# Joining the value products of one tile and the score products of a later one in a single TensorE run, in halves of two PSUM banks

## The chip, the core and the metric

The kernel runs on one core of one Trainium2 chip. The metric is the device time of one execution in microseconds (us). Five engines work from queues of their own, each in order: TensorE (PE) multiplies matrices from SBUF into PSUM, VectorE (DVE), ScalarE (ACT) and GpSimd (POOL) do the element-wise work, SyncE (SP) issues most of the transfers.

## What is computed

Three layers follow each other. The shapes are 8 batches, 8 heads, 576 positions, 64 columns per head; 4608 tokens of 512 columns; hidden widths 1024 and 2048.

```python
# attention inside chunks of 64 positions, q, k, v: (8, 8, 576, 64)
scores = scale * np.matmul(q_c, k_c.transpose(0, 1, 2, 4, 3))
attn = np.exp(scores - np.max(scores, axis=-1, keepdims=True))
attn = attn / (np.sum(attn, axis=-1, keepdims=True) + 1e-09)
x = np.matmul(attn, v_c)                      # then (4608, 512)
# SoLU layer, w_in (512, 1024), w_out (1024, 512)
h = x @ w_in
e = np.exp(h - h_max)
solu = h * (e / (np.sum(e, axis=-1, keepdims=True) + 1e-09))
ln = (solu - mu) / np.sqrt(var + 1e-06) * g_ln
x = ln @ w_out
# leaky layer, w_in (512, 2048), w_out (2048, 512)
h = x @ w_in
out = np.maximum(0.01 * h, h) @ w_out
```

## The kernel before

The first stretch of the kernel does the attention and the SoLU layer in 36 tiles of 128 tokens (`T = 36`); the second does the leaky layer, six groups of 768 tokens, and is not touched. Beside the first stretch, ACT, DVE and POOL also prepare the weights of the later layers piece by piece.

The order of the work is written out by hand: no scheduler moves anything, each engine's queue is in the order in which the loop (L743 to L860) calls the helpers. One round t of the loop (also called tile t below) works on several tiles at once:

- `load_qk(t + 3)` and `load_v(t + 2)` (L756, L757) put transfers on SP's queue.
- `qk_mm(t + 2)` (L347) makes the scores of the tile two ahead: 16 products of 64 x 64 x 64 in the program, 32 records in the trace (s_ps).
- `solu_max(t - 1, 1)` and `solu_a(t - 1)` (L472, L477): row maximum of the second half of the hidden block on DVE (L475), then two exponentials on ACT (L483).
- `softmax_a(t + 2)` (L367): row maximum of the scores (L372) and their subtraction (L373) on DVE, the exponential on ACT (L379).
- `ff1_mm(t, 0)` (L444): first half of the hidden block, 12 products of 512 columns (h_ps, L460). Its last four read the low part of x.
- `solu_b(t - 1)` (L487) on DVE: products L491, which are the last readers of tile t - 1's hidden block. Three PSUM banks hold the halves of hidden blocks in turn, so the second half of tile t gets the bank that the first of these products frees.
- `pt_mm(t + 1)`, `softmax_b(t + 2)`, `pt_copy(t + 1)`: transposes of the probabilities, sum and division, copy on ACT (L402).
- `take_magnitudes`, `convert_a`, `convert_b`: weight pieces, ACT L103, DVE L110 to L120. A round takes one piece, and two in the rounds of `DOUBLE` (5, 6, 7, 14, 15, 22, 23, 30, 31).
- `y1_group` (L552): 24 products of the output of the SoLU layer (y_ps), one group per round from round 5 on.
- `attend(t)` (L580): `pv_mm(t + 1)` (L406) makes the values (x_ps, again 32 records), `x_split(t + 1)` copies their high part on ACT (L437) and makes their low part on DVE (L442).
- `lnT_mm(t - 2)` and `lnT_split` (L525, L541): eight transposes of the normalised block, and their high (ACT L546) and low (DVE L550) parts. These PSUM banks (tag "ef", two of them) are also those of `y1_group`, in turn.
- `ff1_mm(t, 1)`: second half of the hidden block.
- `finish` (L241): of pairs of converted pieces a block is folded and split (L179 to L198): POOL L191 and L192, DVE L193 and L194, ACT L196, POOL L197.

In every fourth round (5, 9, 13, ... 33; `late` in the code) the transposes of the normalised block come ahead of the second half, and `attend` and the output group come last. Rounds 6 to 8, 10 to 12 and so on have the order above.

Scores and values have PSUM tiles with the same tag, "s", of which there is one, two banks wide (`two_banks`, L78). They take turns: the scores are read by DVE before the values of the same round are made, and the values are read by `x_split` before the next scores.

Of the kernel before, what the change touches and what calls it, by code (L numbers as in the profile page):

```python
# [18 lines left out]
B, H, S, D = 8, 8, 576, 64  # L19
# [4 lines left out]
T = NT // P  # L24
NB = NT // 512
KD = DM // P
# [16 lines left out]
AHEAD = 5  # L43
# [9 lines left out]
def kernel(  # L53
# [21 lines left out]
    def bank(tag, name):  # L75
        return (ps2 if tag == "ef" else ps1).tile([P, 512], F32, tag=tag, name=name)

    def two_banks(name):  # L78
        return ps1.tile([P, 2, 512], F32, tag="s", name=name)
# [210 lines left out]
    def w_load():  # L290
        at = next(w_order, None)
        if at:
            w = ws.tile([P, 2, 2 * P], F32R, tag="w", name="w_s")
            sync.dma_start(out=w.bitcast(F32), in_=wi_d[at[0]][:, w_place[at[1]]])
            w_tiles.append(w)
# [12 lines left out]
    with tc.manual_schedule():  # L308

        with ExitStack() as phase:  # L310
# [17 lines left out]
            def load_qk(t, eng=sync):  # L328
                if t >= T:
                    return  # L330
                qt[t] = pa.tile([P, KD, P], F32, tag="qt", name="qt")
                eng.dma_start(out=qt[t], in_=q[t])
                eng.dma_start(out=kbs[t % 2], in_=k[t])

            def load_v(t):
                if t >= T:
                    return
                for r in range(2):
                    for e in range(2):
                        sync.dma_start(  # L340
                            out=vs[t % 2][r * D : (r + 1) * D, 2 * e : 2 * e + 2],
                            in_=v[t, e * D : (e + 1) * D, r::2],
                        )

            s_ps = {}

            def qk_mm(t):  # L347
                if t == 1:
                    ps = [bank("ef", "s_ps") for e in range(2)]
                    s_ps[t] = ps = [x.rearrange("p (h n) -> p h n", h=H)[:, :KD] for x in ps]  # L350
                else:
                    both = two_banks("s_ps").rearrange("p e (h n) -> p e h n", h=H)[:, :, :KD]
                    s_ps[t], ps = both, [both[:, e] for e in range(2)]
                kb, qq = kbs[t % 2], qt.pop(t)
                for i in range(KD):
                    for e in range(2):
                        r = slice(e * D, (e + 1) * D)
                        for c in range(2):
                            pe.matmul(  # L359
                                ps[e][c * D : (c + 1) * D, i, :],  # L360
                                lhsT=qq[r, i, c * D : (c + 1) * D],
                                rhs=kb[r, i, c, :],
                                start=True,
                                stop=True,
                            )

            def softmax_a(t):  # L367
                ps = s_ps.pop(t)
                sm = st8[t] = pa.tile([P, 2, H], F32, tag="st8", name="st8")
                e = es[t] = pa.tile([P, H, D], F32, tag="es", name="es")  # L370
                top = sm[:, 0].rearrange("p (e i) -> p e i", e=2)
                dve.reduce_max(top, ps, axis=AX)  # L372
                dve.tensor_tensor(  # L373
                    e.rearrange("p (e i) n -> p e i n", e=2),
                    ps,
                    top.unsqueeze(3).to_broadcast([P, 2, KD, D]),
                    op=ALU.subtract,
                )
                act.activation(e, e, AF.Exp, scale=scale)  # L379
# [23 lines left out]

            x_ps = {}

            def pv_mm(t):  # L406
                if t == 1:
                    ps = [bank("ef", "x_ps") for r in range(2)]
                    ps = [x.rearrange("p (a n) -> p a n", a=KD)[:, :2] for x in ps]
                    x_ps[t] = [(r, x) for r, x in enumerate(ps)]  # L410
                else:
                    both = two_banks("x_ps").rearrange("p r (a n) -> p r a n", a=KD)[:, :, :2]
                    ps = [both[:, r] for r in range(2)]
                    x_ps[t] = [(slice(0, 2), both)]
                vv, pp = vs[t % 2], pt.pop(t)
                for a in range(2):
                    for c in range(2):
                        for r in range(2):
                            k = slice(r * D, (r + 1) * D)
                            for e in range(2):  # L420
                                pe.matmul(  # L421
                                    ps[r][e * D : (e + 1) * D, a, c * D : (c + 1) * D],
                                    lhsT=vv[k, 2 * e + a, c],
                                    rhs=pp[k, 2 * e + a, c * D : (c + 1) * D],
                                    start=True,
                                    stop=True,
                                )

            def x_split(t):
                x_hi(t)  # L430
                x_lo(t)

            def x_hi(t):
                x = xs[t] = pa.tile([P, 2, KD, P], F32R, tag="xs", name="xs")
                hi = x[:, 0].rearrange("p (a r) n -> p r a n", a=2)
                for r, ps in x_ps[t]:
                    act.activation(hi[:, r], ps, AF.Copy)  # L437

            def x_lo(t):
                hi, lo = (xs[t][:, e].rearrange("p (a r) n -> p r a n", a=2) for e in range(2))  # L440
                for r, ps in x_ps.pop(t):
                    dve.tensor_tensor(lo[:, r], ps, hi[:, r].bitcast(F32), op=ALU.subtract)  # L442
# [29 lines left out]
            def solu_max(t, n):  # L472
                if n == 0:
                    sol[t] = wk.tile([P, 12], F32, tag="z", bufs=3, name="z")
                dve.reduce_max(sol[t][:, 8 + n : 9 + n], hs[t, n], axis=AX, negate=True)  # L475

            def solu_a(t):  # L477
                z = sol[t]
                dve.tensor_tensor(z[:, 0:1], z[:, 8:9], z[:, 9:10], op=ALU.min)  # L479
                u = us[t] = wk.tile([P, FF1], F32, tag="us", bufs=3, name="us")  # L480
                for n in range(2):
                    c = slice(n * 512, (n + 1) * 512)
                    act.activation(  # L483
                        u[:, c], hs[t, n], AF.Exp, bias=z[:, 0:1], accum_out=z[:, 8 + n : 9 + n]
                    )
# [93 lines left out]

            def attend(t):  # L580

                pv_mm(t + 1)
                x_split(t + 1)


            start = ExitStack()
# [66 lines left out]
            def warm(n):  # L653
                for _ in range(n):
                    pe.transpose(spare[:, :P], ident, ident)

            qk_mm(0)
            load_qk(2)
            load_next(2)
# [12 lines left out]
            magnitude(4)  # L672
            warm(14)
            qk_mm(1)
            maxima(0)
            exponentials(0)
# [10 lines left out]
            pt_copy(0)  # L687
            warm(6)
            pv_mm(0)
            maxima(1)  # L690
            exponentials(1)
# [5 lines left out]
            warm(6)  # L697
            ff1_mm(0, 0)
            qk_mm(2)
            factors(1)  # L700
            high(5)
# [6 lines left out]
            magnitude(8)  # L708
            pt_copy(1)
            pv_mm(1)  # L710
            convert(7)
            low(6)
# [30 lines left out]
            for t in range(1, T + 2):  # L743
                if t == T:
# [8 lines left out]
                        y_load(0, n)  # L753
                    for _ in range(WS):
                        w_load()
                load_qk(t + 3)  # L756
                load_v(t + 2)  # L757
                store_next()
                load_next(owed)
# [8 lines left out]
                    groups = [(NB - 1, m) for m in range(KD)]  # L768
                late = g == 0 or t == T - 1
                pieces = 0 if t < AHEAD or t >= T - 2 else 2 if t in DOUBLE else 1  # L770
                if t + 2 < T:
                    qk_mm(t + 2)
                if 1 <= t <= T:
                    if t < 3:
                        solu_max(t - 1, 0)
                    solu_max(t - 1, 1)
                    solu_a(t - 1)
                if t + 2 < T:
                    softmax_a(t + 2)
                if t > AHEAD and not late:  # L780
                    take_magnitudes(pieces)
# [39 lines left out]
                if groups and not late:  # L821
                    for bm in groups:
                        y1_group(*bm)
                    if t + 1 < T:
                        attend(t)
# [7 lines left out]
                else:  # L833
# [4 lines left out]
                    if t == 1:  # L838
                        ff1_mm(t, 1, (2,))
                        attend(t)  # L840
                        ff1_mm(t, 1, (3,))
                    elif t < T - 1 and not late:
                        attend(t)
# [202 lines left out]
        for g in range(NG):  # L1046
# [17 lines left out]
            for s in range(SLOTS):  # L1064
                p, i = divmod(s, PAIRS)
# [93 lines left out]
```

## Time and profile before

| | |
|---|---|
| median of 3 runs | 1241.79 us (1241.59 to 1242.41) |
| profiled execution | 1242.7 us, span of the profile 1240.9 us |
| mean granted clock of TensorE | 0.994 of full speed |
| busy: PE, DVE, ACT, POOL | 1218.2, 892.8, 572.0, 285.9 us |
| rounds 6 to 33, the stretch of the change | from 87.39 to 477.16 us of the span |
| one round there | 13.91 us, 13.96 us in every fourth |

Times in the trace are in us from the start of the span. A timeline row gives the start, the duration, engine, source line, operation, what is written and read, and how many records follow each other; an idle stretch before it stands in brackets with what ended it. The ends of products on PE are modelled, so starts are compared with starts.

### The profile page before, as it was taken

What the parts mean: (1) busy time and instruction counts of PE and PEld (TensorE: products, weight loads), DVE (VectorE), ACT (ScalarE), POOL (GpSimd) and SP (SyncE); (2) the same over time, 40 slices, a digit from 0 to 9 for tenths busy, and PEclk for the clock granted to TensorE, in tenths of its full rate; (3) what the DMA queues carried; (4) which work ended last, traced back from release to release, by engine and by line L of the source; (5) the groups of instructions that cost most, each with busy time, mean ns of one, the idle gap of its engine ahead of it and who ended that gap; (6) DMA issues with size and microseconds to landing.
All of it is one profiled execution on the core that took longest, in us unless ns stands there. A gap on an engine that the chain in (4) does not pass through costs nothing.

```text
span 1240.9 us, 22946 instructions
## 1 busy us (share of the span) xinstructions
PE 1218.2 (98%) x8554; PEld 1073.5 (87%) x8554; DVE 892.8 (72%) x1536; ACT 572.0 (46%) x1079; POOL 285.9 (23%) x388
## 2 busy tenths in 40 slices
PE   5999999999999999999999999999999999999998
PEld 3778878887887878899889989998999899889987
DVE  7789778878987886436785776577657766775675
ACT  6655546545654555433533442353344333443451
POOL 0266557666765664100000000000000000000000
PEclk8899999999999999999999999999999999999999
DMA  7435465654856574279889888988997898789676
GB/s 251 141 117 156 162 207 186 238 176 165 274 175 210 167 246 145 94 264 303 278 285 315 270 242 297 308 253 264 296 305 240 264 306 294 240 267 295 189 228 197
DMA packets 153790, 288.84 MB, mean 233 GB/s; under 512 B 14288, under 2 KB 63440, under 8 KB 152656
## 3 DMA queue, kind: packets, MB, share of 16 engines
q1 hardware_dynamic: 153312, 286.78, 71.8%
q8 instruction: 69, 1.13, 0.4%
q10 hardware_dynamic: 368, 0.59, 0.1%
q14 instruction: 41, 0.34, 0.1%
HBM read 239.08 MB, written 48.23 MB: 232 GB/s over the span
## 4 chain that ended last, share of the span: by engine, by line
PE 94%; DVE 4%; ACT 1%; DMA 0%; POOL 0%; issue 0%; POOLq 0%
PE h_ps L902 28%; PE o_ps L959 19%; PE y_ps L562 16%; PE h_ps L460 15%; PE o_ps L970 10%; PE ln_ps L535 2%; PE x_ps L421 2%; PE s_ps L359 1%; PE pt_ps L396 1%; DVE wf L116 1%; DVE wf L120 0%; DVE us L491 0%; DVE z L475 0%; DMA raw<-in_w_in 0%; DVE wf L112 0%; DVE wf L110 0%
## 5 line engine op out<-in xcount | busy, mean ns | idle before, releaser
L902 PE MATMUL h_ps<-yo,w_s 128*128 128x384 f32 x2016 | 351.0, 334 | 0.0
L902 PEld LDWEIGHTS h_ps<-yo,w_s 128*128 128x128 f32 x2016 | 349.3, 188 | 0.7
L959 PE MATMUL o_ps<-wo_s,yo 128*128 128x512 f32 (+1 forms) x1016 | 262.9, 393 | 0.0
L460 PE MATMUL h_ps<-wi,xs 128*128 128x512 f32 x864 | 219.9, 404 | 3.5 <-DVE xs L442 2.3
L562 PE MATMUL y_ps<-lnT,wo 128*128 128x512 f32 (+1 forms) x888 | 205.5, 388 | 0.2 <-DVE lnT L550 0.2
L959 PEld LDWEIGHTS o_ps<-wo_s,yo 128*128 128x128 f32 x1016 | 179.0, 188 | 28.7
L460 PEld LDWEIGHTS h_ps<-wi,xs 128*128 128x128 f32 x864 | 158.9, 190 | 38.3 <-DVE xs L442 2.6
L562 PEld LDWEIGHTS y_ps<-lnT,wo 128*128 128x128 f32 x888 | 161.1, 188 | 32.6 <-DVE lnT L550 0.4
L970 PEld LDWEIGHTS o_ps<-wo_s,yo 128*128 128x128 f32 x1008 | 144.6, 188 | 15.6
L273 DVE TENSOR_TENSOR yo<-c,yo 128x768 fp32r<-128x768 f32 x144 | 132.4, 951 | 32.0 <-ACT yo L272 32.0
L970 PE MATMUL o_ps<-wo_s,yo 128*128 128x256 f32 x1008 | 149.7, 283 | 0.0
L881 ACT ACTIVATE c<-h_c 128x384 f32<-128x384 f32 x144 | 72.9, 526 | 127.3 <-DVE h_c L913 127.3
L913 DVE TENSOR_TENSOR h_u<-h_ps,h_p 128x384 f32<-128x384 f32 x96 | 53.2, 554 | 106.7 <-PE h_ps L902 99.9
L272 ACT ACTIVATE yo<-c 128x768 fp32r<-128x768 f32 x144 | 113.0, 835 | 7.1 <-DVE c L943 5.5
L483 ACT ACTIVATE us<-h_ps,z 128x512 f32<-128x512 f32 x72 | 48.7, 682 | 48.9 <-DVE z L479 48.9
L386 POOL TENSOR_TENSOR es<-es,st 128x512 f32<-128x512 f32 x33 | 34.5, 1044 | 154.4 <-ACT pt L402 80.1
L272 ACT ACTIVATE yo<-a 128x768 fp32r<-128x768 f32 x36 | 29.9, 837 | 72.5 <-DVE a L267 72.5
L475 DVE TENSOR_REDUCE z<-h_ps 128x1 f32<-128x512 f32 x72 | 48.9, 681 | 19.7 <-PE h_ps L460 19.6
L913 DVE TENSOR_TENSOR h_c<-h_ps,h_u 128x384 f32<-128x384 f32 x96 | 53.1, 553 | 12.8 <-PE h_ps L902 12.3
L570 ACT ACTIVATE ys<-y_ps 128x512 f32<-128x512 f32 x36 | 21.4, 593 | 87.6 <-PE y_ps L562 86.5
L881 ACT ACTIVATE c<-h_ps 128x384 f32<-128x384 f32 x48 | 23.6, 492 | 76.2 <-PE h_ps L902 76.2
L550 DVE TENSOR_TENSOR lnT<-ln_ps,lnT 128x512 fp32r<-128x512 f32 x72 | 45.9, 680 | 12.4 <-ACT lnT L546 12.4
(86 smaller groups left out, 1399.4 us busy)
## 6 DMA issues: line engine op xcount, KB each, us to landing
w_s<-wi_d SPq DMA_DIRECT2D x336, 256.0 KB, 4.0
wo_s<-wo_d SPq DMA_DIRECT2D x168, 512.0 KB, 4.6
wi_d<-wi SPq DMA_DIRECT2D x8, 1792.0 KB, 6.0
wo_d<-wi SPq DMA_DIRECT2D x8, 1792.0 KB, 7.0
raw<-in_w_out SPq DMA_DIRECT2D x24, 512.0 KB, 6.1
raw<-in_w_in SPq DMA_DIRECT2D x23, 512.0 KB, 5.1
vs<-in_v SPq DMA_DIRECT2D x144, 64.0 KB, 3.8
a<-y_d SPq DMA_DIRECT2D x24, 384.0 KB, 5.2
```

Source lines behind the costliest of these rows:

```text
L272: act.activation(o[:, 0], x, AF.Copy)
L273: dve.tensor_tensor(o[:, 1], x, o[:, 0].bitcast(F32), op=ALU.subtract)
L460: pe.matmul(hs[t, n], lhsT=x[:, a, kk, :], rhs=w[:, b, kk % 2, n, :], start=(kk == 0 and a == 0 and b == 0), stop=(kk == KD - 1 and a == 1),)
L475: dve.reduce_max(sol[t][:, 8 + n : 9 + n], hs[t, n], axis=AX, negate=True)
L483: act.activation(u[:, c], hs[t, n], AF.Exp, bias=z[:, 0:1], accum_out=z[:, 8 + n : 9 + n])
L550: dve.tensor_tensor(dst[:, 1], ps, dst[:, 0].bitcast(F32), op=ALU.subtract)
L562: pe.matmul(ps[:, part], lhsT=w[:, a, kk % 4, m * P : (m + 1) * P], rhs=lnT[:, c, kk, pairs, :][:, part], start=(kk == 0 and a == 0 and c ...
L881: act.activation(blocks[block, j // 2][:, j % 2], src, AF.Prelu, alpha=0.01)
L902: pe.matmul(ps, lhsT=w[:, a, kk * P : (kk + 1) * P], rhs=y[:, c, kk, :], start=(first and kk == 0 and a == 0 and c == 0), stop=(kk == 1 an ...
L913: dve.tensor_tensor(o, ps, x, op=ALU.add)
L959: pe.matmul(ps[:, : 2 * P * (a.stop - a.start)], lhsT=x[:, 0, kk, m * P : (m + 1) * P], rhs=w[:, kk, a].rearrange("p a n -> p (a n)"), sta ...
L970: pe.matmul(sums[p % 2][m][:, : 2 * P], lhsT=x[:, 1, kk, m * P : (m + 1) * P], rhs=w[:, kk, 0], start=False, stop=(i == PAIRS - 1 and kk = ...
```

## The change

From round 5 to round 32, `attend(t)` takes the two banks once, as `xs_ps`. `pv_mm(t + 1)` writes its values in the upper 256 columns of both banks, `qk_mm(t + 3)` right behind it the scores of the tile three ahead in the lower 256. Then come `x_split(t + 1)` and `softmax_a(t + 3)`. The calls of `qk_mm(t + 2)` and `softmax_a(t + 2)` at the head of the round remain for rounds up to 5 only. Queries and keys are loaded one tile earlier from round 6 on, and at round 5 for two tiles.

```diff
-            def qk_mm(t):
+            def qk_mm(t, both=None):
...
-                    both = two_banks("s_ps").rearrange("p e (h n) -> p e h n", h=H)[:, :, :KD]
+                    both = two_banks("s_ps") if both is None else both
+                    both = both.rearrange("p e (h n) -> p e h n", h=H)[:, :, :KD]
...
-            def pv_mm(t):
+            def pv_mm(t, both=None):
...
-                    both = two_banks("x_ps").rearrange("p r (a n) -> p r a n", a=KD)[:, :, :2]
+                    both = two_banks("x_ps") if both is None else both
+                    both = both.rearrange("p r (a n) -> p r a n", a=KD)[:, :, 2:]
...
             def attend(t):
 
-                pv_mm(t + 1)
-                x_split(t + 1)
+                if AHEAD <= t < T - 3:
+                    both = two_banks("xs_ps")
+                    pv_mm(t + 1, both)
+                    qk_mm(t + 3, both)
+                    x_split(t + 1)
+                    softmax_a(t + 3)
+                else:
+                    pv_mm(t + 1)
+                    x_split(t + 1)
...
-                load_qk(t + 3)
+                load_qk(t + 3 if t <= AHEAD else t + 4)
...
-                if t + 2 < T:
+                if t <= AHEAD:
                     qk_mm(t + 2)
+                if t == AHEAD:
+                    load_qk(t + 4)
...
-                if t + 2 < T:
+                if t <= AHEAD:
                     softmax_a(t + 2)
```

PE's queue at the end of round 14 and the start of round 15, before (pt and y belong to round 14, the second group of h_ps to round 15):

```order
L396 MATMUL pt_ps<-ident,es 128x128 x4
L562 MATMUL y_ps<-lnT,wo_831 128x512 x12
L562 MATMUL y_ps<-lnT,wo_960 128x512 x12
L421 MATMUL x_ps<-pt,vs_104 64x64 x16
L535 MATMUL ln_ps<-ident,us 128x128 x8
L460 MATMUL h_ps<-wi_172,xs 128x512 x4
L460 MATMUL h_ps<-wi_353,xs 128x512 x4
L460 MATMUL h_ps<-wi_172,xs 128x512 x2
L460 MATMUL h_ps<-wi_353,xs 128x512 x2
L359 MATMUL s_ps<-kb_102,qt 64x64 x16
L460 MATMUL h_ps<-wi_172,xs 128x512 x4
L460 MATMUL h_ps<-wi_353,xs 128x512 x4
```

and with the change:

```order
L397 MATMUL pt_ps<-ident,es 128x128 x4
L564 MATMUL y_ps<-lnT,wo_831 128x512 x12
L564 MATMUL y_ps<-lnT,wo_960 128x512 x12
L423 MATMUL xs_ps<-pt,vs_104 64x64 x16
L360 MATMUL xs_ps<-kb_102,qt 64x64 x16
L537 MATMUL ln_ps<-ident,us 128x128 x8
L462 MATMUL h_ps<-wi_172,xs 128x512 x4
L462 MATMUL h_ps<-wi_353,xs 128x512 x4
L462 MATMUL h_ps<-wi_172,xs 128x512 x2
L462 MATMUL h_ps<-wi_353,xs 128x512 x2
L462 MATMUL h_ps<-wi_172,xs 128x512 x4
L462 MATMUL h_ps<-wi_353,xs 128x512 x4
```

The scores moved from between the two halves of h_ps to the place right behind the values; the halves now follow each other.

DVE's queue over the same place, from the low part of x to the sum of the probabilities, before:

```order
L442 TENSOR_TENSOR xs<-x_ps,xs 128x2x2x128
L550 TENSOR_TENSOR lnT<-ln_ps,lnT 128x4x128 x2
L193 TENSOR_TENSOR wc<-wf,wc 128x256
L194 TENSOR_TENSOR wc<-wf,wc 128x256
L475 TENSOR_REDUCE z<-h_ps 128x1
L479 TENSOR_TENSOR z<-z 128x1
L372 TENSOR_REDUCE st_2650<-s_ps 128x8
L373 TENSOR_TENSOR es<-s_ps,st_2650 128x512
L491 SCALAR_TENSOR_TENSOR us,z<-h_ps,us 128x512 x2
L500 TENSOR_TENSOR z<-z 128x1
L383 TENSOR_REDUCE st_2650<-es 128x8
```

and with the change:

```order
L444 TENSOR_TENSOR xs<-xs_ps,xs 128x2x2x128
L373 TENSOR_REDUCE st_2591<-xs_ps 128x8
L374 TENSOR_TENSOR es<-xs_ps,st_2591 128x512
L552 TENSOR_TENSOR lnT<-ln_ps,lnT 128x4x128 x2
L193 TENSOR_TENSOR wc<-wf,wc 128x256
L194 TENSOR_TENSOR wc<-wf,wc 128x256
L477 TENSOR_REDUCE z<-h_ps 128x1
L481 TENSOR_TENSOR z<-z 128x1
L493 SCALAR_TENSOR_TENSOR us,z<-h_ps,us 128x512 x2
L502 TENSOR_TENSOR z<-z 128x1
L384 TENSOR_REDUCE st_2591<-es 128x8
```

The maximum and the subtraction of the scores moved from behind the SoLU's maximum to ahead of the low parts of the transposed block.

ACT's queue there, from the copy of the values on, before:

```order
L437 ACTIVATE xs<-x_ps 128x2x2x128
L546 ACTIVATE lnT<-ln_ps 128x4x128 x2
L196 ACTIVATE wi<-wf 128x2x256
L196 ACTIVATE wi<-wf 128x256
L196 ACTIVATE wi<-wc 128x4x256
L483 ACTIVATE us,z<-h_ps,z 128x512 x2
L379 ACTIVATE es<-es 128x512
```

and with the change:

```order
L439 ACTIVATE xs<-xs_ps 128x2x2x128
L380 ACTIVATE es<-es 128x512
L548 ACTIVATE lnT<-ln_ps 128x4x128 x2
L196 ACTIVATE wi<-wf 128x2x256
L196 ACTIVATE wi<-wf 128x256
L196 ACTIVATE wi<-wc 128x4x256
L485 ACTIVATE us,z<-h_ps,z 128x512 x2
```

The exponential of the scores moved from behind the SoLU's exponentials to ahead of the high parts of the transposed block.

## Rows read from the trace of the kernel before

**Rows 1.** The page's part 1: busy us (share of the span) xinstructions.
```profile
PE 1218.2 (98%) x8554; PEld 1073.5 (87%) x8554; DVE 892.8 (72%) x1536; ACT 572.0 (46%) x1079; POOL 285.9 (23%) x388
```
**Rows 2.** The page's part 4: the chain that ended last, by engine.
```profile
PE 94%; DVE 4%; ACT 1%; DMA 0%; POOL 0%; issue 0%; POOLq 0%
```
**Rows 3.** Windows of rounds 14 to 17, 18 to 21: length, engines' busy us, clock, DMA.
```profile
198.78:254.47 55.69, 55.69 (x497) 44.79 (x496) 48.98 (x95) 31.82 (x64) 39.55 (x48) 1.00 0.67 232
254.47:310.17 55.70, 55.70 (x498) 44.80 (x497) 43.12 (x85) 29.03 (x59) 31.92 (x43) 1.00 0.56 180
```
**Rows 4.** Timeline of PE, rounds 13 (a fourth one) to 15: start, duration, work.
```profile
185.44 3.02 PE L460 MATMUL h_ps<-wi,xs 128*128 128x512 f32 x12
...
189.53 3.01 PE L460 MATMUL h_ps<-wi,xs 128*128 128x512 f32 x12
...
208.27 0.69 PE L421 MATMUL x_ps<-pt,vs 64*64 64x64 f32 x32
...
209.75 3.01 PE L460 MATMUL h_ps<-wi,xs 128*128 128x512 f32 x12
212.69 0.69 PE L359 MATMUL s_ps<-kb,qt 64*64 64x64 f32 x32
213.31 3.02 PE L460 MATMUL h_ps<-wi,xs 128*128 128x512 f32 x12
216.17 0.60 PE L396 MATMUL pt_ps<-ident,es 128*128 128x128 f32 x4
...
222.19 0.69 PE L421 MATMUL x_ps<-pt,vs 64*64 64x64 f32 x32
```
**Rows 5.** Timeline of PE from 240.83 and from 241.0: parts of one score run.
```profile
240.62 0.59 PE L359 MATMUL s_ps<-kb,qt 64*64 64x64 f32 x28
...
240.79 0.41 PE L359 MATMUL s_ps<-kb,qt 64*64 64x64 f32 x16
```
**Rows 6.** Timeline of PE in rounds 34 and 35, which have no scores.
```profile
487.40 5.73 PE L460 MATMUL h_ps<-wi,xs 128*128 128x512 f32 x24
492.97 1.03 PE L535 MATMUL ln_ps<-ident,us 128*128 128x128 f32 x8
```
**Rows 7.** Timeline of DVE, from round 14's attend to round 16's conversion.
```profile
209.75 0.69 DVE L442 TENSOR_TENSOR xs<-x_ps,xs 128x512 fp32r<-128x512 f32 x1 [1.09 <-ACT xs L437]
...
211.56 1.43 DVE L193 TENSOR_TENSOR wc<-wf,wc 128x256 f32<-128x256 f32 x1
...
213.78 0.68 DVE L475 TENSOR_REDUCE z<-h_ps 128x1 f32<-128x512 f32 x1
...
214.57 0.69 DVE L372 TENSOR_REDUCE st<-s_ps 128x8 f32<-128x512 f32 x1
...
215.89 0.68 DVE L491 SCALAR_TENSOR_TENSOR us<-h_ps,us 128x512 f32<-128x512 f32 x1
...
218.46 1.58 DVE L110 TENSOR_SCALAR wf<-wf 128x512 f32<-128x512 f32 x2
...
223.04 0.68 DVE L475 TENSOR_REDUCE z<-h_ps 128x1 f32<-128x512 f32 x1
...
232.56 0.38 DVE L110 TENSOR_SCALAR wf<-wf 128x512 f32<-128x512 f32 x1
...
235.51 0.68 DVE L475 TENSOR_REDUCE z<-h_ps 128x1 f32<-128x512 f32 x1
```
**Rows 8.** Timeline of ACT over round 14's attend and round 15.
```profile
209.11 0.61 ACT L437 ACTIVATE xs<-x_ps 128x512 fp32r<-128x512 f32 x1
209.60 1.09 ACT L546 ACTIVATE lnT<-ln_ps 128x512 fp32r<-128x512 f32 x2
...
217.87 0.60 ACT L402 ACTIVATE pt<-pt_ps 128x512 f32<-128x512 f32 x1
```
**Rows 9.** Timeline of DVE in round 35, which has no softmax.
```profile
490.45 0.69 DVE L475 TENSOR_REDUCE z<-h_ps 128x1 f32<-128x512 f32 x1 [1.25 <-PE h_ps L460]
...
492.18 0.69 DVE L491 SCALAR_TENSOR_TENSOR us<-h_ps,us 128x512 f32<-128x512 f32 x1 [0.84 <-ACT us L483]
```

## The prediction

> **What bounds the kernel now.** I read the busy shares first: TensorE (PE) is busy for 98% of the span, VectorE (DVE) for 72% [rows 1], and the chain that ended last is PE for 94% [rows 2]. So the length of PE's own queue sets the time, until another engine makes it wait. Next the windows of four tiles [rows 3]: PE is busy in all of both, while VectorE does 48.98 us in the first (tiles 14 to 17) and 43.12 in the second (18 to 21), out of 55.69. VectorE has 6.7 us to spare in the first and 12.6 in the second; the first has two weight pieces in tiles 14 and 15, the second one in each tile. Then PE's timeline [rows 4], where the reader should see two short 64-wide runs in every tile, scores (s_ps) and values (x_ps), each between long 128-wide groups. Last VectorE and ScalarE (ACT) over the same tile [rows 7, 8], since they fill and free PE's buffers.
>
> Letters for a tile: X is the start of its value run, F that of the second half of the first layer behind it, H that of the first half in the next tile, S the VectorE row maximum of the second half.
>
> **What the removed run is worth.** 24 hidden matmuls in one piece take from 487.40 to 492.97, 5.57 us [rows 6]. With the score run between the halves they take from 209.75 to 216.17, 6.42 us [rows 4]. The run costs 0.85 us. Its own work is 32 records in eight groups of four; 12 records lie between 240.62 and 240.79, so a group takes 0.058 and the run 0.47 [rows 5]. The other 0.38 is the change into the 64-wide form and back. The change joins 28 such runs (tiles 5 to 32) to the value runs, so PE's queue gets 28 x 0.38 = **10.6 us** shorter, provided that the scores follow the values at the same pace. I take that: form and quarters of the array are the same, and keys and queries are asked for one tile ahead of their run as before, so I cost the moved loads, one pair ahead of two weight loads on SP's queue at tile 5 included, at nothing. At worst the join costs what a change of form costs, and nothing is saved; more than 0.38 it can't save.
>
> **What the move costs elsewhere.** No work is added, but three things change place.
>
> (a) Values and scores lie in one tile of two banks, and the copies of the values stand behind both products, so I take it that they wait for the last score. The first copy started 0.84 after X (209.11 against 208.27) [rows 4, 8]; now 0.84 + 0.47 = 1.31.
>
> The Trainium skill, "PSUM — Partial Sum Buffer", section "PSUM bank collisions raise a hardware error", says that two engines must not be in one bank at once, disjoint columns included, which is why this wait can't be dropped. No run here shows a collision. If columns did keep the engines apart, the sum below would be some 3 us lower.
>
> (b) The maximum and the subtraction of the scores (1.32 us, 214.57 to 215.89 [rows 7]) leave the place where VectorE waited for the exponentials of the SoLU anyway, and stand ahead of the low halves of the transposed block (lnT); on ACT the scores' exponential stands ahead of the high halves. Step by step after X: first copy 1.31, x low half 1.95 (0.64 later, as 209.11 to 209.75), maximum 2.56, exponential 4.0 (the 1.32 and a hand-over of 0.1), first high half 4.5 (ACT steps by 0.49 from 209.11 to 209.60 [rows 8]), first low half 5.14, both done **X + 6.35**. Before it was 211.56 - 208.27 = X + 3.29 [rows 4, 7]. VectorE idles some 1.25 us of that.
>
> (c) Where these two stood, VectorE now waits for the exponential: 490.45 to 492.18, 1.73 us from S to the first product (L491), the end of the kernel showing this order already [rows 9], against 213.78 to 215.89, 2.11 [rows 7]. That gives back 0.38, but 0.9 of it is idle.
>
> What is late next? H comes at X + 1.48 + 0.47 + 2.8 = X + 4.75 (the halves now in one piece), and the next X 8.77 later (222.19 - 213.31 [rows 4] less the 0.11 of a first weight load). So a tile takes 13.52 instead of 13.92. If weight blocks are folded there (2.22 us, 211.56 to 213.78), S is at X + 8.57, **H + 3.8**; it was H + 0.47. Without them H + 1.6.
>
> *Blocks with one piece per tile* (10 to 13, 18 to 21, 26 to 29). Folding falls in the second tile, so in the third S is at H + 3.8. From S: 1.87 to L491 (ACT's copy of the folded block costs 0.14 more), 2.57 to the conversion (215.89 to 218.46 [rows 7]), 2.95 for one piece (232.56 to 235.51), 0.6 for the first maximum: x's low half at H + 11.8, when it could start at H + 10.7. The rest of its chain takes 4.4, to H + 16.2; the next S is at H + 2.7, the first product ends at 2.7 + 1.73 + 0.7 = H + 5.1. In the fourth tile the transposes come early and F stands at H + 4.0 (189.53 - 185.44 less 0.1 [rows 4]); it needs the bank that this product frees. PE waits **1.2**. In other tiles F comes only at H + 10.7.
>
> *Blocks with two pieces in two tiles* (14 to 17, 22 to 25, 30 to 33). In the second tile S is at H + 3.8, the conversion takes 4.58 (218.46 to 223.04 [rows 7]), so x's low half comes at H + 13.4, 2.7 late. In the third tile the output group needs the bank of the first low half, free at H + 3.8 instead of H + 3.1: 0.7. S is at H + 6.5; the copy of pt, which the values need, started 4.09 after S (217.87 [rows 8]), with the scores' exponential (0.5) and a second piece's copy (0.6) ahead of it that are gone here; so it runs from H + 9.5 to H + 10.1, and the value run waits 0.7 more. In the fourth tile the bank of lnT (0.3, with 0.1 before) and the F wait (2.1) follow: **3.9** in all.
>
> *First block* (6 to 9): two pieces in 6 and 7, no folding, but POOL scales pieces and ACT waits for it. The nearest block is that with two pieces; without its folding, I take 2.4, between 0 and 3.9.
>
> Sum: 3 x 1.2 + 3 x 3.9 + 2.4 = 17.7 us of new waits against 10.6 saved: **7.1 slower**. Made against the profiled execution, 1242.7 (span 1240.9 and 1.8 around it), it gives 1249.8; that execution is 0.9 over the median of the runs shown, 1241.8, so I expect a median of **1248.9**.
>
> Bounds of the waits. Below: VectorE's budget. A two-piece block needs 48.98 + 3 x 2.15 + 0.9 = 56.3 us, and four shortened tiles are 54.2, so 2.1 are missing even if every other idle moment is used; a one-piece block (43.12 + 7.35 = 50.5) misses nothing. Three times 2.1 = 6.3, or 1241.8 - 10.6 + 6.3 = 1237.5. Above: the first block at 3.9, and each late step a tenth longer per tile, about 22, or 1253.
>
> **Rivals.**
> 1. *Faster.* The lateness stays hidden: VectorE's spare time takes it, and PE waits only where the budget is short, if at all. For it: PE shows no wait at all in these tiles now, and the mean budget is enough in half of the blocks. Against it: F's bank in the fourth tile is a fixed date. It decides whether S there is before H + 1.5; for that the low halves must be done by X + 5.2, not X + 6.35. Price: 1231.2 (nothing waits) to 1237.5.
> 2. *No difference.* Only two-piece blocks wait, 3 x 3.9 = 11.7 against 10.6: 1242.9. It needs one-piece blocks to gain 1.2 on my chain, four steps of 0.3.
> 3. *The join saves nothing*: the scores wait in their own way behind the values (a load, a weight load that isn't hidden). Then 17.7 less what the longer tiles hide, some 10: about 1252 or more. Against it: within a run the groups of four follow at 0.058 [rows 5].
>
> **How the numbers follow.** My forecast (waits of 13 to 22 us) has a chance of 0.59, the first rival 0.18, the second 0.18, the third 0.05. The forecast and rival 3 are slower. A measurement of this kernel can tell about 0.2%, 2.5 us, from no change. So faster 0.18, same 0.18, slower 0.64. The range, 1236 to 1254, leaves out most of the first rival and the tail above; the forecast alone is 1245 to 1253.
>
> **What would show it.** PE: 28 joined runs of 64 records without a gap, hidden groups of 24, tiles of about 13.5 us where nothing waits. VectorE: about 1 us idle before lnT's low halves (on ACT's high half) and 0.9 before L491's line in tiles 6 to 33. PE waits on VectorE's us (L491) in tiles 13, 17, 21, 25, 29 and 33, about 1 us in the one-piece and 2 to 3 us in the two-piece blocks. I am wrong if these tiles show no wait, if the value run starts late because of keys, or if the joined run is longer than 1.1 us.

## The result

The changed kernel takes 1253.58 us (median; 1251.52 to 1254.64), the one before 1242.10 beside it (1241.39 to 1242.74). The ratio is 1.009, with a 95% interval of 1.0077 to 1.0103: slower, by 11.5 us where 7.1 were forecast. The profiled execution has a span of 1252.4 us against 1240.9.

Busy shares and the chain that ended last, after:

```profile
PE 1214.1 (97%) x8554; PEld 1074.5 (86%) x8554; DVE 895.5 (71%) x1536; ACT 573.1 (46%) x1079; POOL 284.1 (23%) x388
```
```profile
PE 78%; DVE 14%; ACT 3%; DMA 2%; issue 1%; POOL 1%; SPq 0%; ACTq 0%; POOLq 0%
```

Against [rows 1, 2], PE's busy time is 4 us less and the span 11.5 longer. The busy time falls by less than the 10.6 us that the join saves, since it counts part of the delays as work (the ends of products are modelled). In run 1 below, where PE doesn't wait, it is 1206.7, 11.5 less. PE's part of the chain falls from 94% to 78%, VectorE's rises from 4% to 14%: PE now waits for VectorE. What PE waits for, by line (total us, times, longest us; the rows left out are waits at the start of the kernel):

```profile
PE h_ps L462 <- DVE us L493: 8.4, 6, 1.7
...
PE y_ps L564 <- DVE lnT L552: 2.0, 4, 0.6
PE y_ps L564 <- POOL wo L127: 1.9, 3, 0.8
PE xs_ps L423 <- ACT pt L403: 1.8, 3, 0.6
...
PE y_ps L564 <- ACT wo L126: 0.8, 1, 0.8
PE ln_ps L537 <- ACT ys L572: 0.5, 3, 0.2
```

The first row is the second half of the first layer in the fourth tiles, six of them. The rows on lnT, pt and ys are the third tiles of the two-piece blocks (but for one of the four on lnT, 0.2 us, which stands behind the last tile and is in the kernel before too). The two on wo, the weights of the output groups, lie in the first block, and the prediction had no such wait.

**Where nothing waits** the join does what was forecast. PE in rounds 19 to 21, a block with one piece per tile:

```profile
275.91 0.60 PE L397 MATMUL pt_ps<-ident,es 128*128 128x128 f32 x4
...
281.90 0.69 PE L423 MATMUL xs_ps<-pt,vs 64*64 64x64 f32 x32
282.42 0.65 PE L360 MATMUL xs_ps<-kb,qt 64*64 64x64 f32 x32
283.00 1.09 PE L537 MATMUL ln_ps<-ident,us 128*128 128x128 f32 x8
...
289.42 0.60 PE L397 MATMUL pt_ps<-ident,es 128*128 128x128 f32 x4
...
303.37 1.04 PE L537 MATMUL ln_ps<-ident,us 128*128 128x128 f32 x8
305.54 2.81 PE L462 MATMUL h_ps<-wi,xs 128*128 128x512 f32 x11 [1.13 <-DVE us L493]
```

Values and scores together take 1.10 us (281.90 to 283.00), and the tile 13.51 (275.91 to 289.42) where 13.52 were expected. The last row is the wait in the fourth tile.

VectorE and ScalarE in the same rounds:

```profile
283.76 0.69 DVE L444 TENSOR_TENSOR xs<-xs_ps,xs 128x512 fp32r<-128x512 f32 x1 [1.23 <-ACT xs L439]
284.37 0.68 DVE L373 TENSOR_REDUCE st<-xs_ps 128x8 f32<-128x512 f32 x1
...
287.02 1.29 DVE L552 TENSOR_TENSOR lnT<-ln_ps,lnT 128x512 fp32r<-128x512 f32 x2 [1.24 <-ACT lnT L548]
288.23 1.41 DVE L193 TENSOR_TENSOR wc<-wf,wc 128x256 f32<-128x256 f32 x1
...
290.44 0.68 DVE L477 TENSOR_REDUCE z<-h_ps 128x1 f32<-128x512 f32 x1
...
292.37 0.69 DVE L493 SCALAR_TENSOR_TENSOR us<-h_ps,us 128x512 f32<-128x512 f32 x1 [1.06 <-ACT us L485]
...
304.78 0.69 DVE L493 SCALAR_TENSOR_TENSOR us<-h_ps,us 128x512 f32<-128x512 f32 x1 [0.85 <-ACT us L485]
```
```profile
283.13 0.60 ACT L439 ACTIVATE xs<-xs_ps 128x512 fp32r<-128x512 f32 x1 [0.53 <-PE xs_ps L360]
285.87 0.63 ACT L380 ACTIVATE es<-es 128x512 f32<-128x512 f32 x1 [2.14 <-DVE es L374]
286.41 1.07 ACT L548 ACTIVATE lnT<-ln_ps 128x512 fp32r<-128x512 f32 x2
```

Read from X = 281.90, each step of (a) and (b) can be compared. First copy X + 1.23 (1.31 forecast), released by the last score; x's low half 1.86 (1.95); the maximum 2.47 (2.56); the exponential 3.97 (4.0); first high half 4.51 (4.5); first low half 5.12 (5.14), behind 1.24 of idle time; both done at 288.23, X + 6.33 (6.35). S is at 290.44, X + 8.54 (8.57).

### The profile page after: what moved, and what is told of

It reads as the page before. It is cut to its first block, busy times and chain, and to the rows that moved or that the text cites. A ratio compares the mean times of both kernels' runs of the same rounds, so it can differ in the third digit from the quotient of the medians.

```text
span 1252.4 us, 22880 instructions
## 1 busy us (share of the span) xinstructions
PE 1214.1 (97%) x8554; PEld 1074.5 (86%) x8554; DVE 895.5 (71%) x1536; ACT 573.1 (46%) x1079; POOL 284.1 (23%) x388
## 4 chain that ended last, share of the span: by engine, by line
PE 78%; DVE 14%; ACT 3%; DMA 2%; issue 1%; POOL 1%; SPq 0%; ACTq 0%; POOLq 0%
PE h_ps L913 28%; PE o_ps L970 19%; PE y_ps L564 11%; PE o_ps L981 10%; PE h_ps L462 7%; DVE us L493 2%; DVE lnT L552 1%; DVE wf L116 1%; DVE wf L120 1%; DVE z L477 1%; DVE es L374 1%; DVE xs L444 1%; PE xs_ps L423 1%; DVE wf L110 1%; DVE st L373 1%
## 5 line engine op out<-in xcount | busy, mean ns | idle before, releaser
L462 PE MATMUL h_ps<-wi,xs 128*128 128x512 f32 x864 | 214.6, 402 | 12.0 <-DVE us L493 8.4
L462 PEld LDWEIGHTS h_ps<-wi,xs 128*128 128x128 f32 x864 | 162.3, 192 | 48.0 <-DVE us L493 9.8
L493 DVE SCALAR_TENSOR_TENSOR us<-h_ps,us 128x512 f32<-128x512 f32 x72 | 48.6, 691 | 32.7 <-ACT us L485 32.7
L552 DVE TENSOR_TENSOR lnT<-ln_ps,lnT 128x512 fp32r<-128x512 f32 x72 | 45.8, 680 | 33.8 <-ACT lnT L548 33.8
L380 ACT ACTIVATE es<-es 128x512 f32<-128x512 f32 x33 | 20.9, 632 | 86.7 <-DVE es L374 86.7
```

The lines of the kernel that those rows point to most:

```text
L462: pe.matmul(hs[t, n], lhsT=x[:, a, kk, :], rhs=w[:, b, kk % 2, n, :], start=(kk == 0 and a == 0 and b == 0), stop=(kk == KD - 1 and a == 1),)
L493: dve.scalar_tensor_tensor(u[:, c], hs.pop((t, n)), 1.0 / FF1, u[:, c], op0=ALU.mult, op1=ALU.mult, accum_out=z[:, 10 + n : 11 + n],)
L552: dve.tensor_tensor(dst[:, 1], ps, dst[:, 0].bitcast(F32), op=ALU.subtract)
```

## The experiments

The question: does the join cost the time, or the place to which the softmax's start was moved with it? And within the latter: VectorE's work, ScalarE's order, or the bubble behind the row maximum?

**1. The join alone.** In `attend`, and at the head of the round:

```diff
                     x_split(t + 1)
-                    softmax_a(t + 3)
...
-                if t <= AHEAD:
+                if t + 2 < T:
                     softmax_a(t + 2)
```

> The scores stay in the joined run behind the values, but their softmax goes back to the head of the next round, where VectorE and ScalarE did it before. Theory (the join saves about 10.6 us, and the loss comes from maximum, subtraction and exponential standing ahead of the transposed block's halves): about 10.5 us under the kernel before, 1231.5 (1230 to 1234); PE's waits on VectorE's us in the fourth tiles gone or under 0.3 us each, VectorE's 1.2 us of idle time before the low halves back to under 0.4. Rival (the joined run itself costs it: the value copies wait for the last score, 0.47 us later, and that alone makes VectorE late): 1243 to 1251, waits of 1 us and more in the fourth tiles stay.

Measured: 1231.51 us, ratio to before 0.9917 (0.9901 to 0.9932). PE's waits behind the start-up shrink to one row, which the kernel before has too, and VectorE's on the two lines that idled after the change were 33.8 and 32.7 us there and are now:

```profile
PE y_ps L564 <- DVE lnT L552: 0.2, 1, 0.2
```
```profile
DVE lnT L552 <- ACT lnT L548: 8.7, 2, 8.2
...
DVE us L493 <- ACT us L485: 6.4, 11, 1.5
```

The join is worth what was forecast, 10.6 us (10.9 by the medians), and the value copies' wait for the last score, which is here as well, costs nothing by itself. What made the change slow is the move of the softmax's start. This version takes less time than either kernel.

**2. Only ScalarE's exponential behind the transposed block.** `softmax_a` is cut in two; the maximum and the subtraction stay where the change put them.

```diff
-                act.activation(e, e, AF.Exp, scale=scale)
+
+            def softmax_e(t):
+                act.activation(es[t], es[t], AF.Exp, scale=scale)
...
                         lnT_split(t - 2, 1)
+                    if AHEAD < t < T - 3:
+                        softmax_e(t + 3)
                     if t < T:
                         ff1_mm(t, 1)
```

In late rounds the call stands behind `attend(t)`, and at the head of rounds up to 5 behind `softmax_a`.

> As the changed kernel, but ScalarE's exponential of the scores is issued behind its copies of the transposed block, and only VectorE's maximum and subtraction stay ahead of the halves. Theory (the exponential on ScalarE is the longer part of the 3 us by which the low halves are late: without it the maximum and subtraction fill time in which VectorE would wait anyway): about 8 to 9 us under the kernel before, 1233 to 1236, waits in the fourth tiles near 0. Rival (VectorE's 1.3 us of work at that place are what matters, not ScalarE's order): within 3 us of the changed kernel, 1250 to 1254. Rival (the bubble of 0.9 us behind the row maximum, which stays here, is what matters): 1243 to 1250.

Measured: 1234.63, ratio 0.9938 (0.9925 to 0.9952). No fourth tile waits. VectorE waits behind the row maximum as long as before this edit (34.8 us in all, 32.7 in the changed kernel), so that bubble has no price of its own. What is left are PE's waits for weights in round 6; behind them 22 products take 6.90 us:

```profile
90.54 0.73 PE L566 MATMUL y_ps<-lnT,wo 128*128 128x512 f32 x2 [0.76 <-ACT wo L126]
92.11 6.90 PE L566 MATMUL y_ps<-lnT,wo 128*128 128x512 f32 x22 [0.85 <-POOL wo L127]
```

In the next run, with the same two waits, they took 5.29. The granted clock was 0.50 from 94 to 96 us here and 1.00 there.

**3. The whole softmax start behind the transposed block.** `softmax_a(t + 3)` moves to behind `lnT_split(t - 2, 1)`; in late rounds it stays last.

> As the changed kernel, but the whole softmax start (maximum, subtraction, exponential) stands behind the transposed block's halves in the same tile. Theory: the low halves come about 3 us earlier, the row maximum of the next tile about 1.7 us earlier; 1233 to 1236, waits in the fourth tiles of two-piece blocks under 0.5 us, apart from the last, about 1 us. Rival (the joined run's later value copies or the 0.9 us bubble cost it): 1243 to 1251.

Measured: 1234.87, ratio 0.9939 (0.9925 to 0.9953). No fourth tile waits, the last one neither, where I had expected about 1 us. Like run 2 it keeps the waits for weights in the first block, 2.0 us, and nothing else over 0.2.

**4. The join from round 9 on.** A constant `JOIN = 9` takes the place of `AHEAD` in the five conditions of the change.

> As the changed kernel, but the joined run begins with tile 10 (joins from round 9 on, four fewer). Theory (the first block loses 3.7 us by waits, 2.6 of them of the output group for pieces of its own weights that are converted later, and saves 1.5): some 2 us faster than the changed kernel, 1250.5 to 1252; no wait of the output groups for the weights. Rival (these waits come from somewhere else and only move on): the block of tiles 10 to 13 takes them over, and the time stays at 1253 to 1255.

Measured: 1249.97, ratio 1.0066 (1.0054 to 1.0079): 3.6 us faster than the changed kernel by the medians, 3.0 by the ratios, where some 2 were expected. The waits for weights are gone, the other blocks wait as after the change. This profile shows no stretch at a lower clock in rounds 6 to 33, where that of the changed kernel lost 1.6 us to one (below); that this makes up the rest is likely, but not shown for the other executions behind the medians.

**5. The first block.** In round 5, a late one, the change puts the softmax of tile 8 ahead of ScalarE's magnitudes (L103) of the first two weight pieces. ScalarE after the change, and in run 1, which has it at its old place:

```profile
82.31 0.60 ACT L439 ACTIVATE xs<-xs_ps 128x512 fp32r<-128x512 f32 x1 [1.99 <-PE xs_ps L360]
84.99 0.63 ACT L380 ACTIVATE es<-es 128x512 f32<-128x512 f32 x1 [2.08 <-DVE es L374]
85.53 1.21 ACT L103 ACTIVATE wf<-raw 128x512 f32<-128x512 f32 x2
91.21 0.63 ACT L126 ACTIVATE wo<-wf 128x512 fp32r<-128x512 f32 x1 [4.47 <-POOL wf L173]
```
```profile
80.83 0.60 ACT L439 ACTIVATE xs<-xs_ps 128x512 fp32r<-128x512 f32 x1 [2.00 <-PE xs_ps L360]
81.33 1.24 ACT L103 ACTIVATE wf<-raw 128x512 f32<-128x512 f32 x2
87.12 0.63 ACT L126 ACTIVATE wo<-wf 128x512 fp32r<-128x512 f32 x1 [4.55 <-POOL wf L173]
```

From the copy of x to the magnitudes it is 3.22 us instead of 0.50, and the weights of the output group follow 2.6 later. VectorE's conversion of the pieces (L110) waits for these magnitudes; after the change and in run 1:

```profile
86.21 0.99 DVE L110 TENSOR_SCALAR wf<-wf 128x512 f32<-128x512 f32 x2 [1.25 <-ACT wf L103]
```
```profile
82.07 1.04 DVE L110 TENSOR_SCALAR wf<-wf 128x512 f32<-128x512 f32 x2
```

Counted from x's low half (82.94 and 81.46), it starts 2.7 later: 1.25 of that is the wait in brackets, the rest VectorE's own maximum and subtraction of the scores, which stand ahead of it as well. The run moves this one softmax back, all three operations:

```diff
                     x_split(t + 1)
-                    softmax_a(t + 3)
+                    if t > AHEAD:
+                        softmax_a(t + 3)
...
-                if t <= AHEAD:
+                if t <= AHEAD + 1:
                     softmax_a(t + 2)
```

> As the changed kernel in all but one place: the softmax start of tile 8 (issued in round 5) goes back to the head of round 6. Theory for the first block (in round 5 the scores' exponential on ScalarE stands ahead of the magnitudes of the first two pieces, so these start 2 us late and the output groups of rounds 6 to 8 wait for their own weights, 2.6 us): these waits are gone, about 1 us of lateness stays, 1250 to 1251.5. Rival (the pieces are late because VectorE is late in the block as a whole): the waits for the weights stay within 0.5 us of 2.6, 1253 to 1254.

Measured: 1251.74, ratio 1.0081 (1.0064 to 1.0098), 0.24 above the expected stretch. The waits for weights fall from 2.7 us to 0.6, so the rival falls, but they are not gone as the theory had it; 0.6 in round 8 stays:

```profile
PE y_ps L564 <- POOL wo L127: 0.6, 1, 0.6
```

From the transposes of round 6 to those of round 10 the first block takes 55.30 us here (90.51 to 145.81), 57.89 after the change and 54.42 in run 1. So 2.6 of its 3.5 us come from this one softmax, and 0.9 from the moves in the rounds that follow. This profile has 1.6 us at a lower clock in round 25.

**6. Runs 2 and 5 together.**

> As the run with only ScalarE's exponential behind the transposed block's copies, with the softmax start of tile 8 back at the head of round 6 too. Theory: its last waits, 1.6 us for the weights in the first block (and 1.6 us at a lower granted clock behind them in that profile), go; with none left it equals the run in which the softmax is at its old place, 1230.5 to 1232.5. Rival (VectorE's maximum and subtraction at the new place and the 0.9 us bubble cost something of their own): 1233 to 1235.

Measured: 1231.68, ratio 0.9919 (0.9904 to 0.9934), the same as run 1. VectorE in round 15 of this kernel:

```profile
220.52 0.67 DVE L446 TENSOR_TENSOR xs<-xs_ps,xs 128x512 fp32r<-128x512 f32 x1
221.12 0.67 DVE L373 TENSOR_REDUCE st<-xs_ps 128x8 f32<-128x512 f32 x1
...
222.43 1.28 DVE L554 TENSOR_TENSOR lnT<-ln_ps,lnT 128x512 fp32r<-128x512 f32 x2
...
225.40 0.68 DVE L479 TENSOR_REDUCE z<-h_ps 128x1 f32<-128x512 f32 x1
...
227.33 0.69 DVE L495 SCALAR_TENSOR_TENSOR us<-h_ps,us 128x512 f32<-128x512 f32 x1 [1.06 <-ACT us L487]
```

Maximum and subtraction stand ahead of the low halves here, but these follow at once, without the idle 1.2 us, and the bubble of 1.06 behind the row maximum is there. They make VectorE later, but not late: the row maximum of this tile starts 0.47 behind round 16's transposes of pt (224.93), where run 1 has it 1.40 ahead of them and the changed kernel 3.90 behind (234.91 against 231.01). Outside round 5 both are free, and of the move only ScalarE's order cost time: the exponential ahead of the high halves. In round 5 this run, like run 5, moves all three operations back. No run separates them there; by the rows of run 5, VectorE's two and ScalarE's exponential each have about half of the delay.

**7. The exponential behind the transposed block in the third tiles only.** As run 2, but `softmax_e(t + 3)` stays in `attend` unless `t % 4 == 0`.

> As the changed kernel, but ScalarE's exponential stands behind the transposed block's copies in one tile of four only, the third of each block, just ahead of the tile in which the second half of the first layer waits for its bank. Theory (the wait in the fourth tile is made by what stands ahead of the low halves in the third tile): the waits of 1.1 us in the blocks with one piece go to under 0.2; in the blocks with two pieces the fourth tile's wait of 1.7 falls to about 1, and the third tile's waits (0.6 for the low half, 0.6 for the copy of pt, 0.2) stay, since they come from the second; 1244 to 1247.5. Rival (lateness is carried along evenly from the first tile on): the fourth tile's waits fall by about a third everywhere, 1249 to 1251.

Measured: 1244.61, ratio 1.002 (1.0011 to 1.003).

```profile
PE h_ps L464 <- DVE us L495: 2.2, 3, 0.7
PE y_ps L566 <- DVE lnT L554: 2.0, 4, 0.6
PE y_ps L566 <- POOL wo L127: 1.8, 3, 0.8
PE xs_ps L425 <- ACT pt L405: 1.8, 3, 0.6
```

The waits of the one-piece blocks are gone, those of the two-piece blocks fall to 0.7, less than the 1 expected, and the third tiles' waits stay. So the fourth tile's wait is made in the tile ahead of it, all of it in the one-piece blocks and the larger part in the others, and the third tile's in the tiles ahead of that one.

**8. The changed kernel once more.**

> The changed kernel once more. Theory (the fall of the granted clock to 0.54 behind the 1.68 us wait at 477.88 is not part of the order of the instructions): the same waits, and either the same fall, 1253 to 1254.5, or none, then about 1251.5 to 1252.5. Rival (it belongs to that place): the twelve products behind the wait take 4.6 us again.

Measured: 1253.65 in a single execution, span 1251.8. Behind the start-up each row of PE's waits is the same, but the slow products are elsewhere. The fourth tiles of rounds 25 and 33 in the first profile, then that of round 25 in this one:

```profile
363.95 3.02 PE L462 MATMUL h_ps<-wi,xs 128*128 128x512 f32 x12 [1.68 <-DVE us L493]
...
477.88 4.61 PE L462 MATMUL h_ps<-wi,xs 128*128 128x512 f32 x12 [1.68 <-DVE us L493]
```
```profile
363.33 4.61 PE L462 MATMUL h_ps<-wi,xs 128*128 128x512 f32 x12 [1.68 <-DVE us L493]
```

Each of the two executions has one such place, worth 1.6 us, and the same order of instructions has it at different ones. The rival falls.

## Why the prediction was right, and where its sum was short

Direction and mechanism held, and the size was 4.4 us short. The median lies 0.4 us inside the range, three of its six executions lie above it, and it is 0.6 over the 1245 to 1253 that was given to the forecast alone. By the number, the third rival (about 1252 or more) fits as well; the rows of PE and run 1 set it aside. The profiles after and of run 1 have the same queue on PE, so the difference in the time that a block takes shows what it waits. A block is measured from its first transposes of pt to those of the next one: 90.53 to 148.42 in the first block after, 89.05 to 143.47 in run 1, 57.89 less 54.42.

| rounds | forecast, us | measured, us |
|---|---|---|
| 6 to 9, first block | 2.4 | 3.5 |
| 10 to 13, 18 to 21, 26 to 29, one piece | 1.2 each | 1.4 each |
| 14 to 17, 22 to 25, two pieces | 3.9 each | 4.2 each |
| 30 to 33, two pieces | 3.9 | 4.2, and 1.6 at a lower clock |
| sum | 17.7 | 21.9 |

The medians agree: 1253.58 - 1231.51 = 22.1.

- **The join saves 28 x 0.38 = 10.6.** Right: 1242.41 - 1231.51 = 10.9 by the medians of run 1. Its profile gains 1.52 in each of the five blocks from round 10 to 29, four times 0.38. The third rival (the join saves nothing) falls.
- **(a) The copies wait for the last score.** Right (the first copy is released by L360), but by itself its price is nothing: run 1 keeps the wait and PE waits nowhere for it. What it adds once the softmax is moved too, 3 us by the prediction, was not tried.
- **(b) The softmax ahead of the transposed block.** Right to 0.1 us in every step. Runs 2 and 6 show which half mattered: ScalarE's exponential. VectorE's 1.32 us make the low halves that much later, and outside round 5 that is within what the order bears.
- **(c) The bubble behind the row maximum.** There (1.06 with a folded block, 0.85 without), but free, by run 6.
- **One-piece blocks.** The wait was put at 1.2 and measures 1.4: x's low half of round 20 starts at 298.67, 12.0 behind H (281.90 + 4.75) for 11.8, and the rest of its chain takes the 4.4 that was worked out. The prediction's own terms, H + 5.1 less H + 4.0, give 1.1.
- **Two-piece blocks.** All the waits named are there, and one that was put at 0.1 is 0.4. PE after the change, in round 16, a third tile, and at the wait of round 17:

```profile
231.01 0.60 PE L397 MATMUL pt_ps<-ident,es 128*128 128x128 f32 x4
232.23 5.73 PE L564 MATMUL y_ps<-lnT,wo 128*128 128x512 f32 x24 [0.62 <-DVE lnT L552]
238.58 0.70 PE L423 MATMUL xs_ps<-pt,vs 64*64 64x64 f32 x32 [0.61 <-ACT pt L403]
...
240.50 0.66 PE L537 MATMUL ln_ps<-ident,us 128*128 128x128 f32 x4 [0.17 <-ACT ys L572]
...
249.99 3.02 PE L462 MATMUL h_ps<-wi,xs 128*128 128x512 f32 x12 [1.68 <-DVE us L493]
```

The output group starts 1.22 behind the transposes where 0.35 is usual (275.91 to 276.26 in round 19), 0.87 late for 0.7 forecast. The value run waits 0.7 more for pt's copy, as forecast. The second half of the transposes behind it, for which 0.1 was allowed, comes 0.4 late behind ACT's copy of the output (ys). Against run 1 the third tile is 2.0 us longer, where the terms gave 1.5, and the fourth 2.3, where they gave 2.4. The idle time in brackets is shorter than the delay, because it counts from the modelled end of the products ahead.
- **The first block is the term that was mis-sized most.** "The nearest block is that with two pieces; without its folding, I take 2.4, between 0 and 3.9" looked at the folding and the low halves. It didn't follow the moved softmax through the queues in round 5, a late one, where the magnitudes of the first weights and their conversion stand next. By run 5 that is 2.6 of the 3.5 us; what the prediction had in mind is among the other 0.9. That 2.4 came as near as it did is luck.
- **The clock.** The sum had no term for it: 1.6 us at one of the waits in the profiled execution.
- **The first rival (faster)** missed its deciding point by as much as was said: low halves done at X + 6.33, where X + 5.2 was needed. In run 6 they are done at X + 4.98 (271.58 to 276.56 in round 19), and it comes true: nothing waits.

## What to carry to other kernels

A run moved to save a change of form on one engine takes its followers along on others. For each, go through the queue of the engine to which it goes, in every kind of round, and see what is next in line and who waits for that. Here 10.6 us were there to be had without the followers' move. One instruction of 0.63 us per round, on an engine that is busy for 46% of the span, cost 19 of the 22 us by which the changed kernel is behind run 1 (run 2: 1234.63 against 1253.58).

Busy shares didn't tell which move was harmful. VectorE, the busier engine, bore its two operations for nothing in all rounds but round 5; ScalarE's one, with 2.1 us of idle time ahead of it, was what VectorE waited for.

## What was not expected of the hardware

TensorE's granted clock fell to about half, from its 2.4 GHz level to 1.2, behind one of several equal waits: 4.61 us for twelve products instead of 3.02. Granted clock behind the first profile's waits that end at 249.99 and 477.88 (windows: length, busy us of PE, PEld, DVE, ACT and POOL, clock, DMA share and GB/s):

```profile
250.00:252.00 2.00, 2.00 (x9) 1.66 (x10) 1.90 (x7) 2.00 (x5) 0.00 (x0) 1.00 0.02 6
...
478.00:480.00 2.00, 2.00 (x6) 1.51 (x7) 1.90 (x7) 2.00 (x5) 0.10 (x1) 0.54 0.01 4
```

What the engine did before is the same in both: transposes, 1.68 us without work, then the products; in the two windows of 2 us ahead it was busy for 1.94 and 0.32 us each time. In the second execution and in run 5 the fall came in round 25 instead of 33, in run 4 at no wait in rounds 6 to 33, in run 2 in round 6. The Trainium skill, "TensorE: Matmul & The Clock Gate", section "Part 1: The HAM clock gate (the "warmup" mystery)", says of the start of a kernel that the same one measures different numbers of products at the lower clock from run to run. The executions here differ in the same manner, but in mid-kernel: it is the place of the fall that changes. Why one wait is chosen and another isn't stays open.
